# State updates with 40 columns of k, and the block-by-seven's SBUF-only work on GpSimd for six steps

## The chip, the core and the metric

The kernel runs on one core of one Trainium2 chip. The metric is the device time of one execution in microseconds, lower being better. The names of the engines are those of the profile: PE is TensorE's matmuls, PEld its loads of stationary operands, DVE is VectorE, ACT is ScalarE, POOL is GpSimd, and SP is SyncE, which here only issues DMAs.

## The reference

Two blocks follow each other. The first is an mLSTM cell over 4 batches, 8 heads, 768 steps and a head width of 40. The second is a multiplicative feed-forward block over the 3072 tokens that come out, 320 wide.

```python
for t in range(S):
    m_new = np.maximum(f_gate[:, :, t] + m, i_gate[:, :, t])
    f_stab = np.exp(f_gate[:, :, t] + m - m_new)
    i_stab = np.exp(i_gate[:, :, t] - m_new)
    C = f_stab * C + i_stab * einsum('bhd,bhe->bhde', vt, kt)
    n = f_stab * n + i_stab * kt
    y[:, :, t] = sigmoid(o_gate) * (C @ qt) / maximum(abs(n @ qt), 1)
x = y, with the heads side by side: (3072, 320)
out = ((x @ w1) * (x @ w2)) @ w3 @ w_out
```

The inner width of the feed-forward block is 1024. Everything is float32.

## The kernel before

**The cell in chunks.** The sequence is cut into chunks of 64 steps, and two chunks of one batch (128 tokens, all eight heads) make one unit. There are 24 units, and the main loop's index `s` starts unit `s` and finishes unit `s - 1`; a "step" below is one turn of that loop. Four batches take turns, so that unit `n` is column `n // 4` of batch `n % 4`.

`quarter_work` issues a step's cell matmuls, in this order. For unit `s - 1` come `ph` (masked scores times v) and `pi` (the state before times q). For unit `s` come `ss` (the scores k times q) and `pc`, which is the state update: k, transposed by being the stationary operand, times the weighted v. Each is made of matmuls on a quarter of the 128x128 array, 64 rows by 64 columns. The list `quarters` orders them so that four matmuls in a row use four different quarters. Keys are stored in `kbuf` with 64 columns a head, of which 40 are data and 24 are zeros set once at the start; `vw` has 41 columns a head, v and a one for the normaliser. So `pc` has 64 rows a head, and rows 40 to 63 hold zeros. In the last column of each batch only one of the two chunks needs an update, since no later unit reads the other. `ss` and `pc` lie in one PSUM tile (`cell0`), `pi` and `ph` in another (`cell1`). VectorE then multiplies the scores by the weights (line 388), adds `pc` to the decayed state (lines 395 and 403), and finishes unit `s - 1` (lines 412 to 434, ending with `y`). POOL decays the states (line 331), weights v (line 326) and masks the weights (line 304).

**From y to the feed-forward block.** In later units y goes to DRAM and comes back turned (`send`, `get_back`, `x_turn` at line 461), with DMAs from SP's queue. SP also loads k, v, the output gates, and k and q for a transpose on VectorE (line 313).

**Up.** `w3 @ w_out` is folded into one matrix `w3o`. The products with w1 and w2 are done directly for the first three groups of 512 tokens, and by a scheme with seven products in place of eight for the last three. The second is the block by seven. `weight_sums` (POOL, line 645) and `token_sums` (VectorE, line 652) prepare it once per weight or group. `up_by_seven` then handles one of four column blocks of one group in four parts:

- `single` issues the matmuls that go straight into four PSUM banks, for both weights j = 0 and 1;
- `shared` issues the matmuls that several results share, has ScalarE copy two of them to SBUF (`kept`, lines 688 and 690; the buffer is the memory of `wo`), has VectorE add two more from PSUM (lines 670 and 672), and then forms two sums within SBUF (line 697);
- `left` issues the matmuls with the last 64 rows of x (`wr`), and adds `kept` to the four banks on VectorE (lines 670 and 672 again); the results of j = 0 go to two tiles called `a_sb`, those of j = 1 to `ab`;
- `product` multiplies both within SBUF, in place in `ab` (line 715).

One block runs per step in steps 19 to 30. In steps 19 to 24 it stands beside the cell, and its shared matmuls use the `cell` tiles; from step 25 on the cell is over, and banks come from the pool.

**Down.** `ffn_out` multiplies `ab` by `w3o`; ScalarE copies the result out (line 727) and issues the store.

**Order.** Instructions of an engine run in the order of its queue. Matmuls are tied in the order in which the program issues them (`in_order`). On the other engines a scheduler orders by the program and by dependencies, and `issue_after` holds the block `product`, the transposes and some more behind a given VectorE instruction. The lines below are the ones that issue the last part of a step:

```python
with tc.issue_after(gated.ins) if gated else nullcontext():
    if seven:
        seven[3]()
    if NY <= s - 2 < NU:
        x_turn(s - 2)
```

Of the kernel before, what the change touches and what calls it, by code (L numbers as in the profile page):

```python
# [11 lines left out]
OP = mybir.AluOpType  # L12
# [4 lines left out]
def kernel(  # L17
# [26 lines left out]
    nc = tc.nc  # L44

    B, H, S, D = q.shape
    L = 64
# [3 lines left out]
    NU = NT2 * B  # L51
# [6 lines left out]
    FO = DFF // P  # L58
# [18 lines left out]
    def mps(shape, name):  # L77
        pool = banks.pop(0)
        banks.append(pool)
        return pool.tile(shape, FP, name=name, tag="m")  # L80
# [10 lines left out]
    def mm(out, lhsT, rhs, start=True, stop=True):  # L91
        in_order(nc.tensor.matmul(out, lhsT=lhsT, rhs=rhs, start=start, stop=stop))  # L92
# [9 lines left out]
    halves = [slice(0, L), slice(L, P)]  # L102
# [231 lines left out]
    def quarter_work(s, rest, between):  # L334


        rest()

        def part(j, c0, n):
            return cell[j][:, :, c0:c0 + NP * n].rearrange("p x (n d) -> p x n d", d=n)  # L340

        ss, pc, pi = part(0, 0, L), part(0, NP * L, D1), part(1, 0, D1)
        ph = [cell[1][:, x, NP * D1:2 * NP * D1].rearrange("p (h d) -> p h d", d=D1) for x in range(2)]
        n = s - 1
        if 0 <= n < NU:
            pw, vt, qT = u_t.pop(n), vbuf[n % NBV], qT_t.pop(n)
            before = before_t.pop(n)

            if n < N_DIAG:
                ph = mps([P, H, D1], "ph")  # L350
                for hq in range(H):
                    for r in halves:
                        mm(ph[r, hq, :], pw[r, hq, :], vt[r, hq, :])
            for hd in range(H // 2 if n >= N_DIAG else 0):
                for x, e in quarters:
                    hq = hd if x == e else hd + H // 2
                    mm(ph[x][halves[e], hd, :], pw[halves[x], hq, :], vt[halves[x], hq, :])
            for p in range(NP):
                for hip, x in quarters:
                    mm(pi[halves[x], hip, p, :], qT[heads[hip], p, halves[x]], before[x][heads[hip], p, :])  # L360
        den = None
        if 0 <= s - 1 < NU:
            den = outputs(s - 1, pi, ph)
            den()
            if between:
                for _ in range(3):
                    den()
                den = None
                between()
        n, first_read = s, None  # L370
        if n < NU:
            c, b = divmod(n, B)
            kt, vw = kbuf[n % NB], vw_t.pop(n)
            ends = range(2 if c < NT2 - 1 else 1)
            first, second, after = state[b]
            before_t[n] = first, second
            state[b] = after, second, first
            kT, qT, pw = kT_t.pop(n), qT_t[n], u_t[n]
            for p in range(NP):
                for hip, x in quarters:  # L380
                    mm(ss[halves[x], hip, p, :], kT[heads[hip], p, halves[x]], qT[heads[hip], p, halves[x]])
            for p in range(NP):
                for x, e in quarters:
                    if x in ends:
                        mm(pc[halves[e], x, p, :], kt[halves[x], 2 * p + e, :], vw[halves[x], 2 * p + e, :])
        if n < NU:
            pv = pw.rearrange("p (n two) t -> p two n t", two=2)
            first_read = nc.vector.tensor_tensor(out=pv, in0=ss, in1=pv, op=OP.mult)
        with tc.issue_after(first_read.ins) if first_read else nullcontext():
            if den:  # L390
                den()
            if n < NU:

                if c:
                    nc.vector.tensor_tensor(out=second, in0=pc[:, 0], in1=second, op=OP.add)  # L395
                else:
                    nc.vector.tensor_copy(out=second, in_=pc[:, 0])
                if len(ends) > 1:
                    decayed(after, second, n, 1)
            if den:  # L400
                den()
            if n < NU and len(ends) > 1:
                nc.vector.tensor_tensor(out=after, in0=pc[:, 1], in1=after, op=OP.add)
            if den:
                done = den()
        return done if den else first_read
# [77 lines left out]
    f_sb, a, F, U, on = (gates[0:RG, i * TC:(i + 1) * TC] for i in range(5))  # L484
# [3 lines left out]
    M = const.tile([RG, GC + 1], FP, name="M")  # L488
# [144 lines left out]
    FH, TH = FO // 2, 2 * P  # L633
# [17 lines left out]
        for dst, p, q in ((T1, B12, B11), (T2, B22, T1), (T3, B22, B12), (T4, B21, T2)):  # L651
            nc.vector.tensor_tensor(out=dst, in0=p, in1=q, op=OP.subtract)  # L652

    def up_by_seven(gr, f, bank):


        x, T = x_t[gr], T_t[gr]
        (B11, B12), (B21, B22) = ([x[:, cc, i * TH:(i + 1) * TH] for i in range(2)] for cc in range(KF))
        block, kept = {}, [aside[:, j * 4 * TH:(j + 1) * 4 * TH].rearrange("p (i t) -> p i t", i=4) for j in range(2)]
        lo, hi = (ffn.tile([128, 2, TH], FP, name="a_sb", tag="a_sb") for _ in range(2))  # L660

        def of(j, cc, i):
            return (w1, w2)[j][:, cc, i * CW + f * 128:i * CW + (f + 1) * 128]

        def sum_of(j, i):
            return S_t[j][i][:, f * 128:(f + 1) * 128]

        def add(j, out, p, q):
            if j:
                nc.vector.tensor_tensor(out=out, in0=p, in1=q, op=OP.add)  # L670
            else:
                nc.vector.scalar_tensor_tensor(out=out, in0=p, scalar=UP ** -2, in1=q, op0=OP.mult, op1=OP.add)  # L672

        def single():
            for j in range(2):
                C1, C2 = block[j] = mps([128, 2, TH], "pa"), mps([128, 2, TH], "pb")
                mm(C1[:, 0], of(j, 1, 0), B21, stop=False)
                mm(C1[:, 1], of(j, 1, 1), T[3], start=False, stop=False)
                mm(C2[:, 0], sum_of(j, 3), B22, stop=False)

        def shared():
            p15, p67 = [bank(2 + j) for j in range(2)], [bank(j) for j in range(2)]
            for j in range(2):
                mm(p15[j][:, 0], of(j, 0, 0), B11, stop=False)
                mm(p15[j][:, 1], sum_of(j, 0), T[0], start=False)
            for j in range(2):
                if j:
                    nc.scalar.copy(out=kept[j][:, 0:4:3], in_=p15[j])
                else:
                    nc.scalar.mul(out=kept[j][:, 0:4:3], in_=p15[j], mul=UP ** -2)  # L690
            for j in range(2):
                mm(p67[j][:, 0], sum_of(j, 1), T[1], stop=False)
                mm(p67[j][:, 1], sum_of(j, 2), T[2], start=False)
            for j in range(2):
                for i in range(2):
                    add(j, kept[j][:, 1 + i], p67[j][:, i], kept[j][:, i])
                nc.vector.tensor_tensor(out=kept[j][:, 1:4:2], in0=kept[j][:, 1:3],
                                        in1=kept[j][:, 3:4].to_broadcast([128, 2, TH]), op=OP.add)

        def left():  # L700
            if gr not in ab_t:
                ab_t[gr] = [ffn.tile([128, FO, TH], FP, name="ab", tag="ab", bufs=6) for _ in range(2)]
            for t in range(2):
                for i in range(2):
                    for j, e in quarters:
                        c0 = (f + i * FH) * 128 + e * L
                        mm(block[j][t][halves[e], i], wr[halves[j], c0:c0 + L], x[halves[j], KF, t * TH:(t + 1) * TH],
                           start=False, stop=(i == 1))
            for j, dst in enumerate(((lo, hi), [t[:, f:FO:FH, :] for t in ab_t[gr]])):
                add(j, dst[0], block[j][0], kept[j][:, 0:3:2])  # L710
                add(j, dst[1], block[j][1], kept[j][:, 1:4:2])

        def product():
            for t, a in zip(ab_t[gr], (lo, hi)):
                nc.vector.tensor_tensor(out=t[:, f:FO:FH, :], in0=t[:, f:FO:FH, :], in1=a, op=OP.mult)

        return single, shared, left, product

    def ffn_out(blocks, pos=None):
# [27 lines left out]
    for s in range(len(n_up)):  # L747
# [32 lines left out]
        seven = None  # L780
        if n_seven[s]:
            seven = up_by_seven(*sevens.pop(0), (lambda i: cell[i // 2][:, i % 2].rearrange("p (i t) -> p i t", i=2)) if s <= NU else
                                lambda i: mps([128, 2, TH], "p67" if i < 2 else "p15"))
            if s <= NU:
                seven[0]()
            seven[1]()
# [132 lines left out]
```

## Time and profile before

| | us |
|---|---|
| median of 3 runs | 436.92 (436.5 to 438.46) |
| profiled execution, device time | 436.73 |
| its span, first to last instruction | 435.0 |
| PE busy | 421.6 |
| DVE busy | 306.3 |
| ACT busy | 151.8 |
| POOL busy | 92.8 |
| line 697, mean of 24 | 0.692 |
| line 715, mean of 24 | 0.712 |
| line 645 (same shape, on POOL), means | 1.27 to 1.37 |

The granted TensorE clock was 0.984 over the span. The profile lists engines by the time in which they had at least one instruction running. A row of a group names the source line, the engine, the tiles written and read, the shapes and the count, and after the bar the total busy time, the mean of one instruction in ns, and the idle time of its engine just before. A row of the timeline has start, length, engine, line, tiles, shapes and count; in brackets stands the idle time before it and who ended it. All matmuls carry line 92, where a helper issues them, so they are told apart by their tiles and shapes. Each float32 matmul of the program shows as two loads and two matmuls in the trace.

### The profile page before, as it was taken

How to read it: one execution, taken by the hardware profiler on the slowest of the kernel's cores; microseconds unless marked ns; L12 is line 12 of the kernel's file. 1: busy time of each engine (PE TensorE's matmuls, PEld its weight loads, DVE VectorE, ACT ScalarE, POOL GpSimd, SP SyncE). 2: the span in 40 equal slices, each digit the busy share in tenths (PEclk: the TensorE clock that was granted, in tenths of full speed). 3: DMA queues.
4: the chain of work that ended last, by engine and by line, in shares of the span. 5: the costliest groups of instructions: out<-in, count | busy, mean ns of one | idle time of the engine just before them, and what ended most of it. 6: DMA issues, size and time to landing. Idle time of an engine off the chain costs nothing.

```text
span 435.0 us, 12730 instructions
## 1 busy us (share of the span) xinstructions
PE 421.6 (97%) x5233; PEld 335.1 (77%) x5233; DVE 306.3 (70%) x633; ACT 151.8 (35%) x409; POOL 92.8 (21%) x163
## 2 busy tenths in 40 slices
PE   7699899999999999999999999999999999999996
PEld 6688778878788787887777778788777777777774
DVE  6756886778949778777746968698998876444800
ACT  4866563566724523530332203123211111110110
POOL 4530342333303203303317623022100000000000
PEclk9979799999999999999999999999999999999999
DMA  8999977498987776884426676746221110000001
GB/s 186 213 183 232 222 111 131 126 198 169 205 197 134 171 174 141 173 168 92 102 63 135 151 130 145 160 98 137 53 54 37 35 35 15 17 17 15 2 30 46
DMA packets 135211, 51.14 MB, mean 118 GB/s; under 512 B 109360, under 2 KB 126960, under 8 KB 135152
## 3 DMA queue, kind: packets, MB, share of 16 engines
q1 hardware_dynamic: 131552, 46.29, 51.7%
q10 hardware_dynamic: 3600, 4.03, 2.7%
q8 instruction: 41, 0.67, 0.7%
q14 instruction: 18, 0.15, 0.1%
HBM read 44.50 MB, written 5.80 MB: 116 GB/s over the span
## 4 chain that ended last, share of the span: by engine, by line
PE 71%; SPq 8%; issue 8%; DMA 5%; POOL 3%; DVE 2%; ACT 1%; POOLq 0%; DVEq 0%; ACTq 0%
PE cell L92 19%; PE pa L92 19%; PE pb L92 12%; PE po L92 10%; PE wp L92 6%; PE p L92 5%; SPq L135 4%; DMA raw<-in_moe_w_dram 3%; SPq L180 2%; POOL pw L304 1%; POOL raw L645 1%; SPq L149 1%; SPq L144 1%; DVE w3T L652 1%; PE pt L95 1%
## 5 line engine op out<-in xcount | busy, mean ns | idle before, releaser
L92 PE MATMUL po<-w3o,ab 128*128 128x320 f32 x256 | 70.6, 433 | 0.0
L92 PEld LDWEIGHTS po<-w3o,ab 128*128 128x128 f32 x256 | 48.4, 190 | 19.7 <-issue 0.4
L92 PE MATMUL pa<-xT,w 128*128 128x256 f32 x240 | 61.5, 387 | 1.6 <-ACT xT L475 1.6
L331 POOL TENSOR_TENSOR state<-state,decay 128x164 f32<-128x164 f32 x40 | 19.7, 493 | 168.9 <-DVE state L395 139.2
L92 PEld LDWEIGHTS pa<-xT,w 128*128 128x128 f32 x240 | 45.3, 194 | 9.5 <-ACT xT L475 2.1
L299 ACT ACTIVATE pw<-pw,aT 128x64 f32<-128x64 f32 x184 | 46.4, 339 | 3.3 <-ACT o_sb L727 1.9
L304 POOL TENSOR_SCALAR_AFFINE_SELECT pw<-pw 64x512 f32<-64x512 f32 x48 | 38.2, 796 | 37.0 <-ACT pw L299 24.7
L92 PE MATMUL pb<-xT,w 128*128 128x256 f32 x192 | 45.4, 379 | 0.0
L92 PEld LDWEIGHTS pb<-xT,w 128*128 128x128 f32 x192 | 36.5, 190 | 5.0
L92 PE MATMUL pa<-xT,wr 64*64 64x256 f32 x384 | 37.0, 386 | 0.5 <-DVE wr L196 0.5
L92 PE MATMUL pb<-xT,wr 64*64 64x256 f32 x384 | 36.4, 380 | 0.0
L92 PE MATMUL wp<-wo,w3T 128*128 128x320 f32 x128 | 35.9, 433 | 0.2
L624 ACT ACTIVATE a_sb<-pa 128x512 f32<-128x512 f32 x24 | 14.3, 596 | 61.5 <-PE pb L92 61.5
L92 PE MATMUL cell<-w3o,ab 128*128 128x320 f32 x128 | 35.4, 432 | 0.0
L625 DVE TENSOR_TENSOR ab<-pb,a_sb 128x512 f32<-128x512 f32 x24 | 16.4, 686 | 25.8 <-ACT a_sb L624 25.7
L727 ACT COPY o_sb<-po 128x320 f32<-128x320 f32 x16 | 6.8, 426 | 74.4 <-PE po L92 74.4
L92 PEld LDWEIGHTS cell<-w3o,ab 128*128 128x128 f32 x128 | 24.3, 190 | 9.5
L672 DVE SCALAR_TENSOR_TENSOR a_sb<-pa,wo 128x512 f32<-128x512 f32 x12 | 8.3, 690 | 32.6 <-PE pa L92 32.6
L92 PEld LDWEIGHTS wp<-wo,w3T 128*128 128x128 f32 x128 | 23.8, 190 | 9.6 <-DVE ab L625 0.4
L92 PEld LDWEIGHTS pa<-xT,wr 64*64 64x64 f32 x384 | 18.9, 132 | 15.4 <-issue 8.8
L419 DVE TENSOR_TENSOR h<-cell,h 64x164 f32<-64x164 f32 x88 | 28.7, 326 | 1.7
L92 PEld LDWEIGHTS pb<-xT,wr 64*64 64x64 f32 x384 | 20.1, 133 | 3.0
(141 smaller groups left out, 730.4 us busy)
## 6 DMA issues: line engine op xcount, KB each, us to landing
raw<-in_moe_w_dram SPq DMA_DIRECT2D x64, 128.0 KB, 3.2
kbuf<-in_k_dram SPq DMA_DIRECT2D x24, 160.0 KB, 4.2
vbuf<-in_v_dram SPq DMA_DIRECT2D x24, 160.0 KB, 4.7
o_in<-in_o_gate_dram SPq DMA_DIRECT2D x24, 160.0 KB, 4.8
out_dram<-o_sb ACTq DMA_DIRECT2D x24, 160.0 KB, 1.8
pw<-U_d SPq DMA_DIRECT2D x28, 128.0 KB, 3.6
raw<-in_moe_w_dram SPq DMA_DIRECT2D x5, 512.0 KB, 6.8
raw<-in_moe_w_out_dram SPq DMA_DIRECT2D x8, 320.0 KB, 3.8
```

Of the source, the lines that this page charges most:

```text
L92: in_order(nc.tensor.matmul(out, lhsT=lhsT, rhs=rhs, start=start, stop=stop))
L95: in_order(nc.tensor.transpose(out, in_, ident[0:n, 0:n]))
L135: nc.sync.dma_start(out=dst, in_=rows(src, n))
L180: nc.sync.dma_start(out=dst, in_=src)
L299: nc.scalar.activation(out=pw[:, h, :], in_=src[:, h, :], func=AF.Exp, bias=aT[:, c, b * H + h:b * H + h + 1])
L304: nc.gpsimd.affine_select(out=pw[r], in_=pw[r], compare_op=OP.is_ge, fill=0.0, base=0, pattern=[[0, H], [1, L]], channel_multiplier=-1)
L331: nc.gpsimd.tensor_tensor(out=new, in0=old, op=OP.mult, in1=decay[:, b * NP:(b + 1) * NP, 2 * c + x:2 * c + x + 1] .to_broadcast([P, NP, D1]))
L419: nc.vector.tensor_tensor(out=part, in0=ph[x][halves[e]], in1=part, op=OP.add)
L624: nc.scalar.mul(out=a_sb, in_=pa, mul=UP ** -2)
L625: nc.vector.tensor_tensor(out=ab_t[gr][j][:, fs[0]:fs[-1] + 1, t0:t0 + a_sb.shape[-1]], in0=pb, in1=a_sb, op=OP.mult)
L672: nc.vector.scalar_tensor_tensor(out=out, in0=p, scalar=UP ** -2, in1=q, op0=OP.mult, op1=OP.add)
L727: nc.scalar.copy(out=o_sb, in_=po)
```

## The change

In the state update, every unit but unit 0 takes the first 40 columns of a head's k as the stationary operand, and so writes 40 of the 64 rows of its quarter. Unit 0 still takes 64; it is the one that first fills the tile. The moving operand, the order and the number of matmuls stay. VectorE still reads all 128 rows of `pc`; the rows that are no longer written are not used by any later product.

In the block by seven, an argument chooses the engine for the two sums of line 697 and the two products of line 715. It is GpSimd in steps 19 to 24, VectorE in steps 25 to 30. The arithmetic is the same. The line numbers of the changed kernel are higher by one from the new line on.

```diff
--- before.py
+++ after.py
@@ -379,10 +379,11 @@
             for p in range(NP):
                 for hip, x in quarters:
                     mm(ss[halves[x], hip, p, :], kT[heads[hip], p, halves[x]], qT[heads[hip], p, halves[x]])
+            M = D if n else L
             for p in range(NP):
                 for x, e in quarters:
                     if x in ends:
-                        mm(pc[halves[e], x, p, :], kt[halves[x], 2 * p + e, :], vw[halves[x], 2 * p + e, :])
+                        mm(pc[e * L:e * L + M, x, p, :], kt[halves[x], 2 * p + e, 0:M], vw[halves[x], 2 * p + e, :])
         if n < NU:
             pv = pw.rearrange("p (n two) t -> p two n t", two=2)
             first_read = nc.vector.tensor_tensor(out=pv, in0=ss, in1=pv, op=OP.mult)
@@ -651,7 +652,7 @@
         for dst, p, q in ((T1, B12, B11), (T2, B22, T1), (T3, B22, B12), (T4, B21, T2)):
             nc.vector.tensor_tensor(out=dst, in0=p, in1=q, op=OP.subtract)
 
-    def up_by_seven(gr, f, bank):
+    def up_by_seven(gr, f, bank, aside_by):
 
 
         x, T = x_t[gr], T_t[gr]
@@ -694,7 +695,7 @@
             for j in range(2):
                 for i in range(2):
                     add(j, kept[j][:, 1 + i], p67[j][:, i], kept[j][:, i])
-                nc.vector.tensor_tensor(out=kept[j][:, 1:4:2], in0=kept[j][:, 1:3],
+                aside_by.tensor_tensor(out=kept[j][:, 1:4:2], in0=kept[j][:, 1:3],
                                         in1=kept[j][:, 3:4].to_broadcast([128, 2, TH]), op=OP.add)
 
         def left():
@@ -712,7 +713,7 @@
 
         def product():
             for t, a in zip(ab_t[gr], (lo, hi)):
-                nc.vector.tensor_tensor(out=t[:, f:FO:FH, :], in0=t[:, f:FO:FH, :], in1=a, op=OP.mult)
+                aside_by.tensor_tensor(out=t[:, f:FO:FH, :], in0=t[:, f:FO:FH, :], in1=a, op=OP.mult)
 
         return single, shared, left, product
 
@@ -780,7 +781,7 @@
         seven = None
         if n_seven[s]:
             seven = up_by_seven(*sevens.pop(0), (lambda i: cell[i // 2][:, i % 2].rearrange("p (i t) -> p i t", i=2)) if s <= NU else
-                                lambda i: mps([128, 2, TH], "p67" if i < 2 else "p15"))
+                                lambda i: mps([128, 2, TH], "p67" if i < 2 else "p15"), nc.gpsimd if s <= NU else nc.vector)
             if s <= NU:
                 seven[0]()
             seven[1]()
```

## Prediction

> **What bounds the kernel now.** I read the page's busy rows first, then the slices, then what TensorE waited for, then the groups by shape, and last the timeline of the steps that the change touches. All durations are of one profiled execution: 436.73 us, of which 435.0 us are the span and 1.73 us lie around it. That stands 0.19 us below the median of the runs shown, 436.92 us. About 0.5% (2.18 us) is what a measurement of this kernel can tell from no change, so "faster" below means under 434.7 us.
>
> ```profile
> PE 421.6 (97%) x5233; PEld 335.1 (77%) x5233; DVE 306.3 (70%) x633; ACT 151.8 (35%) x409; POOL 92.8 (21%) x163
> PE   7699899999999999999999999999999999999996
> DVE  6756886778949778777746968698998876444800
> POOL 4530342333303203303317623022100000000000
> PE pa L92 <- ACT xT L475: 0.8, 1, 0.8
> ```
>
> TensorE is busy 97% and in nearly every slice 90% or more; from the span's 88th us on, the waits longer than the listing's threshold add up to 0.8 us (last line). A busy matmul row alone doesn't prove a bound, but matmuls here follow each other with no hole, so what shortens TensorE's own stream shortens the end, unless another engine is right behind. VectorE reaches 9 tenths between 283 and 326 us, inside the six steps at issue (steps 19 to 24, 246 to 340 us), where POOL is at 2 tenths or less. So VectorE is nearly full there, yet it is not what TensorE waits for.
>
> **Part one, 40 columns of k.** The change cuts the stationary operand of the state update from 64 to 40 columns in steps 1 to 23; the moving operand stays 41 wide, and the number of instructions stays.
>
> ```profile
> 161.16 0.56 PEld L92 LDWEIGHTS cell<-qT,kT 40*64 40x64 f32 x32
> 161.19 0.67 PE L92 MATMUL cell<-qT,kT 40*64 40x64 f32 x32
> 161.63 0.56 PEld L92 LDWEIGHTS cell<-vw,kbuf 64*64 64x64 f32 x32
> 161.68 0.63 PE L92 MATMUL cell<-vw,kbuf 64*64 64x41 f32 x32
> 162.24 0.31 PEld L95 LDWEIGHTS px<-ident,y 128*128 128x128 f32 x3
> L92 PEld LDWEIGHTS pu<-ident,gates 96*32 96x32 f32 x32 | 1.0, 110 | 0.3 <-issue 0.3
> L92 PEld LDWEIGHTS cell<-vw,kbuf 64*64 64x64 f32 x704 | 14.0, 139 | 0.2 <-POOL vw L326 0.2
> L92 PEld LDWEIGHTS wp<-wo,w3T 128*128 128x128 f32 x128 | 23.8, 190 | 9.6 <-DVE ab L625 0.4
> ```
>
> The first five lines are one step's batches. 32 instructions are 8 rounds of four quarters side by side. The score batch moves 64 columns, the update only 41, yet both advance at the same pace: the starts of successive rounds are 58 to 59 ns apart in either (read instruction by instruction from the same timeline). So what is equal in both must set the pace: the load of 64 columns. The last three lines give its size: 110, 139 and 190 ns for 32, 64 and 128 columns, about 0.85 ns a column. 58.5 ns is then 64 columns at 0.83 (53 ns) and some 5 ns beside; with 40 columns I estimate 33 + 5 = 38.5 ns. The stream does not take over: a 256-column matmul advances in 216 ns, 0.83 ns a column, so 41 columns need 34 to 37 ns. Of the batch's intervals the first two (41 and 48 ns) are partly the hand-over from the scores and the way out is the next batch's, so five intervals save 20 ns, one 10, and the last load about 10: 0.12 us a step. In the last four updates only two quarters run, 16 instructions, but again in 8 rounds of 58.5 ns (they too take 0.55 us to the next batch), so they save as much.
>
> Against this stands a rule. The Trainium skill, "TensorE: Matmul & The Clock Gate", Back-to-back issue gap, says that matmuls of 1 to 64 columns all cost about 60 cycles, an issue floor; its section on LDWEIGHTS says that a load costs by its columns. The equal pace of 41 and 64 columns is what a floor would show too. By a floor the pace stays 58.5 ns and the time stays 436.7 us; by the load rule it is 0.12 us a step. I take the load, since the three load durations scale and since 60 full-speed cycles are 25 ns, well below 38.5 ns; but no row shows a 40-column load, and zero stays as one bound. The other bound is all eight rounds at 20 ns, 0.16 us.
>
> Which steps keep it? Steps 1 to 3 lie where TensorE waits for DMA, ScalarE and VectorE anyway: no gain. From step 4 on there are 20. Two places take some back, where another chain arrives together with TensorE (chain of waits, then timeline):
>
> ```profile
> 97.02 0.49 PE cell L92 x32
> ...
> 106.70 1.94 DMA gates<-in_q_dram
> ...
> 110.99 0.65 DVE ab L625
> 111.68 8.88 PE wp L92 x32
> ```
> ```profile
> 240.04 0.58 DVE L461 STREAM_TRANSPOSE xT<-yb 128x384 f32<-128x384 f32 x1 [0.35 <-DMA yb<-y_d]
> ...
> 244.29 1.46 POOL L645 TENSOR_TENSOR raw<-w,raw 128x512 f32<-128x512 f32 x1
> ...
> 244.53 1.50 DVE L652 TENSOR_TENSOR w3T<-xT 128x256 f32<-128x256 f32 x1
> ...
> 246.68 0.30 PEld L92 LDWEIGHTS pa<-w3T,w 128*128 128x128 f32 x2 [0.54 <-DVE w3T L652]
> ```
>
> At 111.68 TensorE waits for VectorE, whose chain goes back by DMA and SP's queue to TensorE at 97.5, before the update of step 8: what steps 8 and 9 save is lost, 0.24 us. At 246.68 it waits for the token sums, and that chain goes back by VectorE's transposes, the DMA of `yb` and an SP queue that issues without a pause from 228.6, to the y of step 16 and TensorE at 223.1: what steps 16, 17 and 18 save is lost, 0.35 us. Elsewhere TensorE's waits (62.93, 87.96) follow its own transposes, behind the update, and move with it. Left are 15 steps x 0.12 = 1.8 us.
>
> **Part two, POOL in place of VectorE.** In each of steps 19 to 24, two sums (line 697, 0.69 us each) and two products (line 715, mean 0.71 us) leave VectorE: about 2.7 us a step, 16 us in all, none of it on TensorE's path: it has no wait over the threshold from 246.7 to 340. The nearest row for POOL is line 645, same shape and two SBUF inputs: 1.27 to 1.37 us. So POOL gains 24 instructions, about 5.3 us a step, beside at most 5 us that it has in a step of 14 to 18 us. No DMA is moved; ScalarE's and SP's queues keep their order.
>
> In POOL's queue the sums come after the decay that opens a step, the products after the sums and, from step 20 on, ahead of the next step's `vw`, its two masks and its decay. A product waits only for VectorE's block add (line 670), not for y. Queued behind: `vw` and masks come about 2.6 us later. `vw` is wanted by the update and the mask by line 388, both about a step (14 us) on: hidden, and if that cover were gone, 2.6 us a step. In step 19 alone the second decay stands between sums and products and waits for VectorE as it does now.
>
> The tight place is the sum, which the block adds now await across engines. The tightest step is 22, with the token sums in it:
>
> ```profile
> 305.80 0.42 DVE L652 TENSOR_TENSOR w3T<-xT,w3T 128x256 f32<-128x256 f32 x1
> ...
> 309.24 0.69 DVE L697 TENSOR_TENSOR wo<-wo 128x512 f32<-128x512 f32 x1
> 309.85 0.68 DVE L672 SCALAR_TENSOR_TENSOR a_sb<-pa,wo 128x512 f32<-128x512 f32 x1
> ```
>
> Now VectorE reaches the block adds at 309.85 with no wait for TensorE. After, without 1.3 us of products ahead, its first two adds end about 306.4, POOL's sums about 307.7 and 309.0; the block adds of the first half start when TensorE's `wr` matmuls end, about 309.4, those of the second about 310.7. Cover 1.6 us; behind it the next step's matmuls take the bank only at 311.96, 1.4 us after the first add's end. Three us in all before TensorE waits. The products of step 22 feed the output matmuls at 318.1; they end at about 314.4 in place of 317.6. So part two costs 0.
>
> The rule that speaks against it: the Trainium skill, "SBUF — State Buffer", Who interferes with whom, says that a VectorE instruction with two SBUF inputs and a GpSimd one that reads SBUF exclude each other for their whole length. The trace agrees: line 652 takes 0.42 us alone and 1.37 to 1.50 beside POOL's line 645, which goes from 1.28 to 1.46. By the rule every sum or product could stop VectorE once, 4 x 1.3 = 5.2 us a step against 2.7 relieved, a loss of 2.5 us of VectorE. By place it is less: beside the products stand lines 412, 419 and 388, which read PSUM and one SBUF tile; only lines 432 and 434 meet POOL's delayed `vw` and masks, 0.49 to 0.76 and 0.82 us as in the earlier steps. I take 0.6 us a step, under the 2.7 relieved.
>
> **Sum.** 436.73 - 1.8 - 0 = 434.9 us; with the 0.19 us to the median, 435.0. I forecast 435.0 us, 0.4% less.
>
> **Rivals.** A, all is kept: VectorE's and DMA's chains at 111.68 and 246.68 turn out to have room, or the load saves 0.16 us: 20 x 0.12 to 0.16 = 2.4 to 3.2 us, 433.7 to 434.5 us. For it: waits of 0.1 us are small. Against: what they wait for is not shortened. B, the pace is a floor (or the quarters' issue): nothing, 436.7 us. C, slower: with 40 columns the four quarters no longer load side by side. A round then costs 4 x 38.5 = 154 ns in place of 58.5, 0.76 us a batch of 8 rounds; over the 16 updates of steps 4 to 19 that is 12 us, 449 us. It decides as soon as a round takes over 58.5 ns; over 0.5% is lost from some 75 ns on. Against it: the state batch has 40 rows in quarters of 64 and runs at 58.5 ns; its tile stays 64 x 64. The same side would be reached by POOL's sums coming more than 3 us late, which by the rows above they don't.
>
> **Chances.** Forecast 0.42, A 0.29, B 0.16, C and other losses 0.13. Of the forecast a fifth falls below 434.7. Faster 0.37, same 0.50, slower 0.13. The range of 8 in 10 reaches from A's middle over B to a small loss: 433.6 to 437.8 us.
>
> **What would show it.** Right: the update's load group near 117 ns, the way from its first matmul to the next batch 0.44 us in place of 0.56; sums and products on POOL near 1.3 us; lines 697 and 715 gone from VectorE up to step 24; TensorE's wait at 246.7 grown by some 0.35 us. Wrong: an unchanged 0.56 us (B), a longer one (C), a TensorE wait for VectorE or POOL between 247 and 340 us (part two isn't free), or no larger waits at 111.7 and 246.7 (A).

## The result, and the profile after

The changed kernel took 435.42 us (median of 9 runs, 433.39 to 435.95), beside 436.84 us for the kernel before in the same session (median of 9, 434.27 to 438.46). The ratio over paired runs is 0.995, with a 95% interval from 0.9926 to 0.9974. So it is faster, by about half a per cent.

The profiled execution took 433.39 us, its span 431.7. Against the 436.73 us of the profile before, that is 3.3 us, more than the medians show. Part of it is not the change. In the page's slices, the row of the granted clock was `9979799999999999999999999999999999999999` before: two slices below 9, from about 20.7 to 27.5 and from 48.0 to 54.8 us. After, it has no such slice (below). I therefore compare the two traces from the state update of unit 8 to that of unit 23, where both ran at full clock: 227.45 us before, 225.82 after, 1.63 us less. From the update of unit 23 to the end of the span it is 109.32 and 109.36.

The page of the changed kernel, busy times and slices:

```profile
PE 413.2 (96%) x5233; PEld 326.1 (76%) x5233; DVE 293.5 (68%) x609; ACT 151.7 (35%) x409; POOL 123.1 (29%) x187
PE   6689789999999999999999999999999999999996
DVE  6766886779949778877655948478865876444800
POOL 4630352233303303302327644364643200000000
PEclk9999999999999999999999999999999999999999
```

24 instructions have moved from VectorE to POOL (633 to 609, 163 to 187). Where steps 19 to 24 are, POOL's digits rise from 3 or less to 3 to 6, and VectorE's fall from 6 to 9 to 4 to 8. TensorE's row is nines almost throughout, as before.

What TensorE waits for from the span's 88th us on, in the changed kernel (engine, tile and line of the instruction that waits, what it waits for; us in total, times, longest):

```profile
PE wp L92 <- DVE ab L626: 0.7, 1, 0.7
PE pa L92 <- DVE w3T L653: 0.4, 1, 0.4
```

These are the two places that the prediction named, at 110.07 and 243.87 us of this trace. The wait at the first was 0.12 us before and is 0.70 now; at the second, 0.14 and 0.42. (The wait of 0.8 us for `xT` that the prediction's listing shows is still there, 0.78 us long; it ends at 86.21 us of this trace, just ahead of the window.)

Groups of instructions by shape, changed kernel (tiles, shapes, count; then busy us, mean ns of one; then idle time before them):

```profile
L92 PEld LDWEIGHTS cell<-vw,kbuf 64*40 64x40 f32 x672 | 10.0, 114 | 1.1 <-issue 1.1
L716 POOL TENSOR_TENSOR ab<-ab,a_sb 128x512 f32<-128x512 f32 x12 | 15.3, 1293 | 18.3 <-DVE ab L671 18.3
L698 POOL TENSOR_TENSOR wo<-wo 128x512 f32<-128x512 f32 x12 | 14.9, 1267 | 21.7 <-DVE wo L673 21.7
```

The load of 40 columns takes 114 ns in place of 139. A sum or product on POOL takes 1.27 and 1.29 us in place of VectorE's 0.69 and 0.71. Lines 433 and 435 (432 and 434 before) are VectorE instructions with nothing else than SBUF operands. Their means over all 24 steps rose from 0.69 to 0.72 and from 0.67 to 0.81, but about half of the second rise lies in steps 4 to 8, where no work was moved. Where it was moved, the rise is in steps 19 to 22, half of it in step 19, where both lines meet the products:

```profile
265.65 2.75 POOL L716 TENSOR_TENSOR ab<-ab,a_sb 128x512 f32<-128x512 f32 x2
265.97 1.30 DVE L433 SCALAR_TENSOR_TENSOR o_in<-o_in,den 128x320 f32<-128x320 f32 x1
267.30 1.44 DVE L435 TENSOR_TENSOR y<-h,o_in 128x320 f32<-128x320 f32 x1
```

Before, these two took 0.76 and 0.82 us in that step.

The timeline of one step's cell batches in the changed kernel (start, length, engine, instruction, count):

```profile
159.04 0.67 PE L92 MATMUL cell<-qT,kT 40*64 40x64 f32 x32
159.54 0.49 PE L92 MATMUL cell<-vw,kbuf 64*40 64x41 f32 x32
159.96 0.55 PE L95 MATMUL px<-ident,y 128*128 128x128 f32 x3
```

From the start of the update's row to the start of the row behind it is 0.42 us; before, it was 0.56. Read from the first matmul of one batch to that of the next, it is 422 ns in place of 558 in the steps with four quarters, and 411 in place of 551 in those with two. The starts of the rounds lie 41, 36, 41, 36, 36, 43 and 36 ns apart, 38.4 in the mean of all seven and of the last five. Before, the first two were 41 and 48 ns and the last five 58 to 59.

### The profile page after: what moved, and what is told of

Read it like the earlier page. It is cut to its first block, busy times and chain, and to the rows that moved or that the text cites. A ratio compares the mean times of both kernels' runs of the same rounds, so it can differ in the third digit from the quotient of the medians.

```text
span 431.7 us, 12748 instructions
## 1 busy us (share of the span) xinstructions
PE 413.2 (96%) x5233; PEld 326.1 (76%) x5233; DVE 293.5 (68%) x609; ACT 151.7 (35%) x409; POOL 123.1 (29%) x187
## 4 chain that ended last, share of the span: by engine, by line
PE 43%; issue 29%; POOL 10%; SPq 9%; DVE 4%; DMA 3%; ACT 1%; POOLq 0%; DVEq 0%
PE cell L92 15%; PE po L92 10%; PE pa L92 8%; PE p L92 5%; PE pb L92 5%; POOL pw L304 4%; SPq L135 4%; SPq L180 3%; POOL state L331 2%; POOL vw L326 2%; SPq L149 1%; POOL raw L646 1%; DMA wo<-in_moe_w_dram 1%; DVE w3T L653 1%; DMA raw<-in_moe_w_dram 1%
## 5 line engine op out<-in xcount | busy, mean ns | idle before, releaser
L92 PE MATMUL pa<-xT,w 128*128 128x256 f32 x240 | 60.6, 383 | 1.6 <-ACT xT L476 1.6
```

## The experiments

Three groups of runs; each ran beside the kernel before on its own chip (medians 436.82, 436.37 and 436.94 us). To see where time goes I cut each trace at the starts of the state updates of units 4, 8, 10, 15, 19 and 23, read from TensorE's timeline. The pieces are in us; the text below refers to them.

| kernel | 4 to 8 | 8 to 10 | 10 to 15 | 15 to 19 | 19 to 23 |
|---|---|---|---|---|---|
| before | 47.97 | 32.33 | 77.39 | 56.32 | 61.41 |
| after | 47.15 | 32.47 | 76.45 | 56.05 | 60.85 |
| e1, columns only | 46.83 | 32.46 | 76.50 | 56.04 | 60.85 |
| e2, GpSimd only | 47.08 | 32.37 | 77.45 | 56.33 | 61.40 |
| e3, 32 columns | 46.27 | 32.61 | 77.35 | 56.29 | 61.32 |
| e4, 48 columns | 46.92 | 32.78 | 76.66 | 56.12 | 61.03 |
| e5, changed again | 47.14 | 32.50 | 76.45 | 56.05 | 60.84 |
| e6, weight sums earlier | 47.69 | 32.49 | 76.91 | 55.36 | 60.85 |
| e7, conversion later | 46.87 | 29.72 | 80.96 | 56.07 | 60.85 |
| e8, both | 47.20 | 29.44 | 80.96 | 55.37 | 60.85 |
| e9, columns and weight sums | 46.97 | 32.48 | 76.45 | 55.37 | 60.85 |
| e10, weight sums with GpSimd | 47.58 | 32.49 | 76.44 | 55.37 | 60.85 |
| e11, each sum twice | 47.14 | 32.48 | 76.45 | 56.05 | 61.33 |
| e12, each sum three times | 46.91 | 32.47 | 76.54 | 56.05 | 66.53 |

The first column includes the half-clock window of the profile before, and differs by up to 0.9 us between kernels that are the same there. Nothing is read from it.

### Which of the two parts gains: e1 and e2

e1 leaves the sums and products on VectorE:

```diff
-            ..., nc.gpsimd if s <= NU else nc.vector)
+            ..., nc.vector)
```

> Only the 40 columns; sums and products stay on VectorE. Theory (all the gain is the update's shorter load): the whole gain of the changed kernel, -1.2 to -1.7 us against before; the update's batch takes 0.42 us to the next one, and TensorE waits about 0.6 to 0.7 us near the end of step 8 and about 0.4 us for the token sums. Rival (VectorE's relief in steps 19 to 24 also pays): less gain than the changed kernel by 0.5 us or more, with TensorE waits between 247 and 340 us.

e1 took 434.04 us (12 runs, 433.36 to 435.0), ratio 0.9938 (0.9918 to 0.9959). Every piece from unit 8 on agrees with the changed kernel within 0.05 us. In this kernel, too, TensorE's two waits are there (waits of PE from 88 us on):

```profile
PE pa L92 <- DVE w3T L653: 0.4, 1, 0.4
PE wp L92 <- DVE ab L626: 0.4, 1, 0.4
```

e2 keeps 64 columns and moves the sums and products:

```diff
-            M = D if n else L
+            M = L
```

> Only the sums and products on GpSimd; 64 columns everywhere. Theory: no change, within 0.3 us of before; no TensorE wait over 0.1 us in steps 19 to 24, VectorE waiting longer for TensorE there. Rival (the relief pays): 0.5 us or more faster. Rival (the shared port costs): slower by 0.5 us or more, with TensorE waits in steps 19 to 24.

e2 took 436.9 us (12 runs, 435.25 to 439.37), ratio 1.0018 (0.9995 to 1.0042), and has no TensorE wait over the threshold between 247 and 340 us. So the columns give the whole gain, and the move to GpSimd gives nothing that can be measured.

### Load or floor: e3 and e4

If the load of the stationary operand sets the pace, 48 columns must lie between 40 and 64, and 32 can gain only what the 41-column stream allows; a floor would not care. e3 leaves columns 32 to 39 of k out of the state.

```diff
-            M = D if n else L
+            M = 32 if n else L     # e3
+            M = 48 if n else L     # e4
```

> The changed kernel with 32 columns of k in the update; this leaves columns 32 to 39 of k out of the state. Theory (below some 40 columns the 41-wide stream sets the pace, 34 to 37 ns a round): the batch takes 0.40 to 0.42 us to the next, hardly less than the 0.42 with 40. Rival (the load alone sets the pace, 32 x 0.83 + 5 = 32 ns): 0.37 us.

> The changed kernel with 48 columns of k in the update (8 of them the zeros). Theory (the load's columns set the pace, 48 x 0.83 + 5 = 45 ns a round): the batch takes 0.47 us to the next, between 0.42 with 40 and 0.56 with 64. Rival (the pace steps at multiples of 32 columns): 0.56 us as with 64.

One run each: 434.6 and 435.18 us. The timeline of one step in e3, and then in e4:

```profile
174.46 0.67 PE L92 MATMUL cell<-qT,kT 40*64 40x64 f32 x32
175.07 0.50 PE L92 MATMUL cell<-vw,kbuf 64*32 64x41 f32 x32
175.50 0.33 PE L95 MATMUL px<-ident,y 128*128 128x128 f32 x1
```

```profile
175.72 0.67 PE L92 MATMUL cell<-qT,kT 40*64 40x64 f32 x32
176.21 0.53 PE L92 MATMUL cell<-vw,kbuf 64*48 64x41 f32 x32
176.68 0.33 PE L95 MATMUL px<-ident,y 128*128 128x128 f32 x1
```

With 48 columns the batch takes 464 ns to the next one, between 422 (40) and 558 (64): about 5 ns a column from 40 to 48 and 6 from 48 to 64. The last five rounds lie 45 to 46 ns apart in the mean, where 45 were expected. The recorded load takes 107, 114, 122 and 139 ns for 32, 40, 48 and 64 columns. So from 64 down to 40 the number of columns sets the pace, as a load would; the moving operand was 41 columns wide throughout. With 32 columns the batch takes 431 to 434 ns, no less than with 40; its first two intervals are 52 and 49 ns, and its last five rounds lie 37 ns apart in the mean, hardly less than the 38.4 with 40. So another bound holds there. The theory named the 41-column stream, but no run changed the stream's width, so this stays open. e3 shows a second thing, which neither theory had. The score batch ahead of it starts 0.61 us before the update, not 0.49 or 0.50 as in e4 and in the changed kernel; read by first matmuls, 604 ns in place of 494. With a stationary operand of 64 rows by 32 columns, some 110 ns are lost on the way in, and none with 40 or 48; that the quarters change their shape there, from 64x64 to 64x32, is the likely cause and is not shown. A step is then 15.41 us with 32 columns, 15.29 with 40, 15.33 with 48 and 15.43 with 64. 40 columns are the best of the four.

### Where the savings are lost: e5, e6, e7 and e8

The changed kernel ran again in this group:

> The changed kernel as it is, beside the next three on one chip. Theory (the GpSimd part is free but for some 0.2 us at the very end): -1.5 to -2.5 us against before, as with the 40 columns alone. Rival (the GpSimd part costs about 0.8 us): -1.0 to -1.7 us.

It took 434.35 us (12 runs, 433.97 to 435.87), ratio 0.9961 (0.9938 to 0.9984): 2.0 us less than before by the medians, as the theory had it, though the interval covers the rival too.

The token sums on VectorE (line 653) run beside POOL's last weight sums, and TensorE waits for them at 243.87. Timeline of TensorE before, and then of the changed kernel; the bracket is the idle time before, and what ended it:

```profile
245.84 0.70 PE L92 MATMUL pa<-xT,w 128*128 128x256 f32 x2
246.68 0.70 PE L92 MATMUL pa<-w3T,w 128*128 128x256 f32 x2
```

```profile
239.65 0.73 DVE L653 TENSOR_TENSOR w3T<-xT 128x256 f32<-128x256 f32 x1
240.42 1.38 DVE L653 TENSOR_TENSOR w3T<-xT,w3T 128x256 f32<-128x256 f32 x1
241.47 1.45 POOL L646 TENSOR_TENSOR raw<-w,raw 128x512 f32<-128x512 f32 x1
241.72 1.49 DVE L653 TENSOR_TENSOR w3T<-xT 128x256 f32<-128x256 f32 x1
242.74 0.70 PE L92 MATMUL pa<-xT,w 128*128 128x256 f32 x2
243.13 0.68 DVE L653 TENSOR_TENSOR w3T<-xT,w3T 128x256 f32<-128x256 f32 x1
243.87 0.70 PE L92 MATMUL pa<-w3T,w 128*128 128x256 f32 x2 [0.42 <-DVE w3T L653]
```

e6 takes POOL out of the way by giving both weights' sums one step earlier:

```diff
-        if s in (16, 17):
-            weight_sums(s - 16)
+        if s in (15, 16):
+            weight_sums(s - 15)
```

> The changed kernel with the two blocks of weight sums (line 646, GpSimd) one step earlier, in steps 15 and 16, so that none runs beside the token sums. Theory (the savings of steps 16 to 18 are lost because the token sums hold TensorE, and these are long because the weight sums on GpSimd lock the port): token sums 0.42 us each, TensorE's 0.4 us wait for them gone, 0.3 to 0.5 us faster than the changed kernel. Rival (the chain by the DMA of yb and the transposes holds it, whatever the token sums take): the wait stays at 0.3 to 0.4 us.

Timeline of e6 at the same place:

```profile
242.75 0.41 DVE L653 TENSOR_TENSOR w3T<-xT 128x256 f32<-128x256 f32 x1
...
243.88 0.42 DVE L653 TENSOR_TENSOR w3T<-xT,w3T 128x256 f32<-128x256 f32 x1
246.07 0.70 PE L92 MATMUL pa<-xT,w 128*128 128x256 f32 x2
246.61 0.59 PE L92 MATMUL pa<-w3T,w 128*128 128x256 f32 x2
```

Each token sum is 0.41 to 0.43 us long in place of 0.68 to 1.49, and the matmul has no bracket any more: it starts 0.54 us after the one ahead of it, where the changed kernel needs 1.13 and the kernel before 0.84. Units 15 to 19 take 0.69 us less than in the changed kernel. The whole took 433.94 us (12 runs, 432.92 to 436.29), ratio 0.9953 (0.9931 to 0.9974): the gain in the piece is clear, that in the whole is within the spread of the runs.

e7 tries the first place, at 110 us. It moves one conversion of a half tile of `w3` (with its VectorE transpose, line 244, 1.13 us long, which runs directly ahead of the late products of line 626) from step 8 to step 9:

```diff
-    n_cvt = [0, 0, 2, 0, 1, 2, 3, 3, 3] + [2] * 6
+    n_cvt = [0, 0, 2, 0, 1, 2, 3, 3, 2, 3] + [2] * 5
```

> The changed kernel with one of the three weight conversions that step 8 does on VectorE moved to step 9. Theory (the savings of steps 8 and 9 are lost to VectorE, whose three conversions stand ahead of the product that frees a bank for TensorE): TensorE's wait of 0.4 to 0.7 us near the end of step 9 gone, and 0.3 to 0.7 us faster than the changed kernel. Rival (a DMA or TensorE's own order takes its place): the two steps stay at 32.4 us from the update of unit 8 to that of unit 10.

This made it worse: 435.75 us (12 runs, 433.69 to 437.64), ratio 0.9981 (0.9957 to 1.0004), slower than the changed kernel in the same group. Units 8 to 10 take 2.75 us less, but 10 to 15 take 4.51 more, together 1.76 us more. The waits of PE from 88 us on in e7:

```profile
PE pa L92 <- ACT xT L476: 2.7, 2, 1.9
```

The wait for `ab` is gone, and a wait of 1.95 us for ScalarE's copy of the next `xT` stands at 117.60 (the other 0.78 us of the line is the wait at 87.88 that every kernel has). The reason is in TensorE's timeline, of the changed kernel and then of e7:

```profile
110.07 8.88 PE L92 MATMUL wp<-wo,w3T 128*128 128x320 f32 x32 [0.69 <-DVE ab L626]
128.96 0.49 PE L92 MATMUL cell<-vw,kbuf 64*40 64x41 f32 x32
129.76 4.47 PE L92 MATMUL wp<-wo,w3T 128*128 128x320 f32 x16
```

```profile
111.18 4.47 PE L92 MATMUL wp<-wo,w3T 128*128 128x320 f32 x16
127.88 0.49 PE L92 MATMUL cell<-vw,kbuf 64*40 64x41 f32 x32
128.68 8.78 PE L92 MATMUL wp<-wo,w3T 128*128 128x320 f32 x32
```

The conversion took a whole fold of `w3` with it: 16 rows, 4.4 us of TensorE's work, went from ahead of the update of unit 10 to behind it. That moves 4.4 us from one piece to the next. Most of the net loss is the new wait: without those 4.4 us of work TensorE reaches the next matmuls on `xT` early and stands for 1.95 us. The work that was moved had covered a longer wait than the 0.7 us that the edit removed.

e8 has the edits of e6 and e7 together.

> The changed kernel with both of these. Theory: the gains add, 0.7 to 1.1 us faster than the changed kernel, about -3 us against before. Rival: one wait takes the place of the other and the sum is no more than the better of the two.

436.55 us (12 runs, 433.28 to 438.23), ratio 0.999 (0.9963 to 1.0016). The pieces are e7's up to 15 and e6's behind it. The wait at 117.95 is 1.31 us here.

### Is the GpSimd part worth its place: e9 and e10

e9 is e6 with the sums and products on VectorE; e10 is e6 again, beside it on the same chip.

> The 40 columns and the earlier weight sums, sums and products on VectorE. Theory (the GpSimd part is worth nothing, and costs 0.2 us at the end): -2.5 to -3 us against before, and 0.1 to 0.5 us better than the same with the GpSimd part. Rival (the relief of VectorE pays once TensorE is faster): worse than the same with the GpSimd part by 0.3 us or more.

> The same with the GpSimd part (the changed kernel with earlier weight sums, a second time), beside the kernel above on one chip. Theory: -2 to -2.8 us against before; the profiled execution ends 0.18 us later after the last matmul than the kernel above. Rival: as above, the other sign.

e9: 433.73 us (7 runs, 432.4 to 435.71), ratio 0.9931 (0.9907 to 0.9956). e10: 433.59 us (6 runs, 431.52 to 435.16), ratio 0.9927 (0.9899 to 0.9954). They are equal, and both beat the kernel before, by 0.7%. Against the changed kernel, which wasn't in that group, the gain is shown by the piece from 15 to 19, not by the medians.

### How much cover the sums have: e11 and e12

e11 and e12 give each sum on POOL one or two extra instructions of its size ahead of it. Each writes a half of `a_sb` that the block add overwrites, so the result is not changed.

```diff
+                if aside_by is nc.gpsimd:
+                    for _ in range(1):     # e11; range(2) in e12
+                        aside_by.tensor_tensor(out=lo, in0=kept[j][:, 1:3],
+                                               in1=kept[j][:, 1:3], op=OP.add)
                 aside_by.tensor_tensor(out=kept[j][:, 1:4:2], ...
```

> The changed kernel with one more sum of the same shape on GpSimd ahead of each of the two sums in steps 19 to 24 (its result goes to a tile that the block adds overwrite), so that the sums land about 1.3 and 2.5 us later. Theory (the cover is some 3 us): steps 20 to 23 stay at 60.85 us from the update of unit 19 to that of unit 23, within 0.3 us; VectorE's wait for TensorE before the block adds shrinks. Rival (the block adds had no room): 1.3 us a step, 66 us.

> The same with two more sums ahead of each, so that the second sum lands about 5 us later. Theory (past some 3 us TensorE waits for the banks): 1 to 3 us a step in steps 21 to 23, 63 to 69 us from the update of unit 19 to that of unit 23, and TensorE waits for VectorE's block adds. Rival (no limit yet): 60.9 us.

One run each: 436.94 and 441.42 us. Units 19 to 23 take 0.48 us more in e11 and 5.68 more in e12 than in the changed kernel. POOL's timeline in step 22 of e12:

```profile
306.51 2.16 POOL L700 TENSOR_TENSOR a_sb<-wo 128x512 f32<-128x512 f32 x2 [4.33 <-DVE wo L673]
308.75 1.27 POOL L701 TENSOR_TENSOR wo<-wo 128x512 f32<-128x512 f32 x1
```

An extra sum takes 1.04 to 1.08 us, so that the two sums of a step end about 1.1 and 2.2 us later in e11, 2.2 and 4.3 us later in e12. But the extras delay something else as well. The first block add (`a_sb<-pa`) writes the half of `a_sb` that they write, so it waits for all of them, those ahead of the second sum too. It reads nothing that the sums write. VectorE and TensorE in the same step of e12, and then the row of a window from 312.9 to 316.4 us (its length, busy us of PE, PEld, DVE, ACT and POOL, granted clock, DMA share, GB/s):

```profile
309.97 2.16 POOL L700 TENSOR_TENSOR a_sb<-wo 128x512 f32<-128x512 f32 x2
312.16 0.69 DVE L673 SCALAR_TENSOR_TENSOR a_sb<-pa,wo 128x512 f32<-128x512 f32 x1 [4.94 <-POOL a_sb L700]
312.91 1.16 PE L92 MATMUL pa<-xT,w 128*128 128x256 f32 x2 [2.07 <-DVE a_sb L673]
```

```profile
312.90:316.40 3.50, 3.49 (x8) 2.80 (x9) 3.42 (x8) 0.00 (x0) 2.85 (x3) 0.51 0.00 0
```

So TensorE's 2.07 us are the price of a late first block add, and not of a late sum. In the changed kernel this add starts 2.37 us ahead of the matmul that takes its bank again and lasts 0.69, so it has about 1.7 us to spare. In e11 it starts 1.1 us later against that matmul, and TensorE does not wait for it; in e12 3.8 us later, and 2.1 come through. Behind that wait the granted clock was at half for 3.4 us, which cost about 1.7 us more in the same step. (e7's wait of 1.95 us had no such stretch behind it; no run tells why.)

In e11 TensorE's only wait over the threshold here is 0.21 us at 314.39, for VectorE's line 420. The loss of 0.48 us is more than the 0.3 that was allowed and far from the rival's 5. The cover of the sums themselves is measured by neither run. The next section estimates it from the changed kernel's trace.

## Why the prediction was right, point by point

**The pace.** The estimate was 38.5 ns a round, and 38.4 was measured. The rule that spoke against it, an issue floor for up to 64 columns (the Trainium skill, "TensorE: Matmul & The Clock Gate", Back-to-back issue gap), did not set the pace of these rounds of four quarters: with 41 moving columns throughout, the batch took 558, 464 and 422 ns for loads of 64, 48 and 40 columns. As the cause of the 58.5 ns it would have given no gain; the 25 ns that the prediction worked out from it lie below every pace measured here, so the runs do not test that figure. The load rule of the same page gave the gain that came. Rivals B and C fall with it.

**The saving of a step.** 0.12 us were estimated; the way to the next batch became 0.136 us shorter, 0.140 where two quarters run. The five full intervals saved 100 ns, as estimated; the last round with the way out saved 24 ns in place of 10, and the first two intervals 12 in place of 10. Where nothing takes it back, the pieces agree: four steps from 19 to 23 are 0.56 us shorter, 4 x 0.136 = 0.54.

**Where it is lost.** This step held in place and less well in size.

| stretch | steps x 0.136 | measured | lost |
|---|---|---|---|
| 8 to 10 | -0.27 | +0.14 | 0.41 (0.24 predicted) |
| 10 to 15 | -0.68 | -0.94 | none |
| 15 to 19 | -0.54 | -0.27 | 0.27 (0.35 predicted) |
| 19 to 23 | -0.54 | -0.56 | none |

In the stretch from 10 to 15, the 0.26 us beyond the steps' own saving are not the change's. One step, from unit 11 to 12, took 15.69 us in the profile before, 0.26 more than its neighbours. e6 and e10 are the same kernel, and this step took 15.74 us in the one profile and 15.29 in the other. So this stall comes and goes from run to run, and the two profiles compared here happen to differ in it.

At the first place the waits vary by run: 0.70 us in the changed kernel's profile, 0.36 in e1 after 0.12 at 99.61, and in e5 0.40 at 99.76 with 0.11 there. The piece is steadier, 32.46 to 32.50 us in every profile with 40 columns but e7 and e8. Its loss of 0.41 us is three steps' saving, where the prediction counted two. The chain of the changed kernel would allow that: traced back from the `ab` that TensorE waits for, it lies in DMAs and in VectorE's, ScalarE's and SP's queues down to 79.9 us, ahead of the updates of units 7, 8 and 9, while the prediction's left TensorE at 97.5, ahead of unit 8's alone. That this is the cause is not shown; with 48 columns, which save less, the piece took longer still, 32.78 us.

**Why it is lost at the token sums.** Here the prediction's reason was incomplete, although its number was near. It led the chain back by VectorE's transposes and the DMA of `yb` to the y of step 16, and took the length of the token sums as given. e6 moved only POOL's weight sums, and the wait was gone. Against the update of unit 17 its token sums start 0.2 us earlier and end 2.8 us earlier, because all four together take 1.55 us in place of 4.16. So the chain reached TensorE only with its last link made long: VectorE and POOL exclude each other in SBUF, which the prediction had measured itself (0.42 against 1.37 to 1.50 us) but used only for part two. With that out of the way, units 15 to 19 take 0.95 us less than before: the four steps' 0.54, and 0.41 us of delay that was there from the start (0.30 between the two matmuls shown above, 0.11 behind them).

**Part two.** It was costed at nothing on TensorE's path, and e2 and the pair e9 and e10 show so. By its terms: POOL's rows were taken at 1.27 to 1.37 us, and measured 1.27 and 1.29. VectorE was busy 84.0 us from 240 to 340 us before, 72.1 after; 2.0 us a step by six steps, where 2.7 - 0.6 = 2.1 was predicted. In steps 20 to 22 line 433 took 0.55 us (0.76 allowed) and line 435 took 0.82 (0.82), in steps 23 and 24 both took 0.49. Step 19 went otherwise. The prediction placed lines 412, 419 and 388 beside the products; in step 19, where the second decay delays the products, lines 433 and 435 met them and took 1.30 and 1.44 us, 1.16 us more than before. TensorE did not wait for them. Where the time of VectorE went, the trace shows; waits of DVE from 240 to 340 us, before and then after:

```profile
DVE a_sb L672 <- PE pa L92: 9.3, 5, 3.2
```

```profile
DVE a_sb L673 <- PE pa L92: 19.4, 6, 5.3
```

VectorE got free and waits longer for TensorE; no run shows another use of the relief. Step 22 went as worked out; timeline of the changed kernel:

```profile
303.82 0.87 DVE L671 TENSOR_TENSOR wo<-cell,wo 128x256 f32<-128x256 f32 x2
304.05 2.50 POOL L698 TENSOR_TENSOR wo<-wo 128x512 f32<-128x512 f32 x2 [4.41 <-DVE wo L673]
306.22 0.69 DVE L673 SCALAR_TENSOR_TENSOR a_sb<-pa,wo 128x512 f32<-128x512 f32 x1 [1.52 <-PE pa L92]
308.29 0.68 DVE L671 TENSOR_TENSOR ab<-pb,wo 128x512 f32<-128x512 f32 x1
308.45 2.50 POOL L716 TENSOR_TENSOR ab<-ab,a_sb 128x512 f32<-128x512 f32 x2 [1.90 <-DVE ab L671]
309.41 1.34 DVE L420 TENSOR_TENSOR h<-cell,h 64x164 f32<-64x164 f32 x4
311.28 0.59 PE L92 MATMUL cell<-xT,w 128*128 128x256 f32 x2
```

POOL starts its sums beside VectorE's last adds and ends at 306.55, when VectorE, idle for 1.52 us, has just got TensorE's result. The products start 2.2 us after the first block add. The cover was put at three us, up to the `pa` bank. Another path is tighter. The second sum ends at 306.55 and VectorE reads it in `ab<-pb` at 308.29, 1.7 us later; from there VectorE runs without a pause through line 420, which ends at 310.75, 0.5 us before TensorE takes that `cell` tile at 311.28. That makes about 2.3 us, an estimate from this one step, and e11's one wait of TensorE is on this path.

**The end.** The tail was costed at nothing and is 0.18 us longer: from the last matmul's start to the end of the span 3.75 us before, in e1 and in e9, and 3.93 in the changed kernel, e2 and e10. It goes with the GpSimd part, and the prediction had no term for it.

**The sum.** From unit 8 to unit 23 the trace gives -1.63 us. The prediction has for that stretch 15 steps less the five that it counted lost, 10 x 0.12 = 1.2 us, and 1.8 with the steps ahead of unit 8 and the last update. That the sum came out so near is in part luck. The bigger saving per step adds 0.24 us and the stall that only the profile before had 0.26; the bigger loss at steps 8 and 9 takes 0.17. Without that stall the stretch gives about 1.4 us. Steps 4 to 7, 0.48 us of the sum, can't be told: that piece varies more between runs than they are worth. Rival A, all savings kept, is refuted: in e6 the second place is kept and the wait there is gone; the changed kernel has both waits, longer than before.

## What to carry to other kernels

When small matmuls run side by side, compare the pace of batches that differ in only one size: what equally fast batches share is the candidate, and a run that changes it decides. Here the stationary operand's zero padding was paid for until it was as narrow as the moving operand. Relieving an engine that nothing waits for moves its idle time and not the end, and a slower engine may take its work as long as the cover (here about 2.3 us by estimate) is not used up. An instruction put in to measure cover must write where nothing else on the path waits for it; in e11 and e12 it did not. Behind a small saving on the bound engine, look next at the places where another chain arrives with it: one stall by two engines excluding each other in SBUF took back two steps' savings, and a reordering that changed neither engine's amount of work gave them back, with 0.4 us more. A piece in which one profile differs from the next should be looked up in a second profile of the same kernel before it is put down to a change.

## What the runs showed of the hardware that was not expected

- Behind the score batch, an update with 32 columns cost TensorE about 110 ns on the way in (604 ns from one batch to the other in place of 494), which made 32 columns worse than 40. A change of the quarters' shape is the likely cause.
- Of two POOL additions of 128x512 elements, the extra one of e11 and e12, whose two inputs are the same slice, took 1.04 to 1.08 us, and the sum itself, whose second input is another slice broadcast, 1.27. No run separates the cause: the output's place differs, too.
- The end of the span comes 0.18 us later in each kernel with the sums and products on GpSimd, though no GpSimd instruction stands near: ScalarE's closing instruction comes about 0.27 us later. No run tells why.
- After a wait of 2.07 us in e12 the granted clock was 0.5 for 3.4 us. It is the only such stretch behind unit 8 and ahead of the last matmuls in all these profiles; waits of 1.95 us (e7) and 1.31 us (e8) had none.
